# Output projection of an attention block: two fp32 products a tile in place of six products of high and low parts

## The chip, the cores and the metric

The kernel runs on one core of a Trainium2 chip. The metric is device time of one execution in microseconds. The profile shows one execution, its engines (PE is TensorE's matmul, PEld its load of weights, DVE VectorE, ACT ScalarE, POOL GpSimd, SP the queue that issues DMAs) and the granted clock of TensorE.

## What is computed

Three layers on 8 x 576 tokens of width 512: chunked attention in 8 heads, a mixture of four attention experts of head size 64, and a normed MLP. The change touches the second one; from its reference:

```python
for e in range(E):
    q = x @ wq[e]; k = x @ wk[e]; v = x @ wv[e]
    scores = scale * (q @ k.transpose(0, 2, 1))
    scores = np.where(causal, -1000000000.0, scores)
    scores = scores - scores.max(-1, keepdims=True)
    a = np.exp(scores)
    a /= a.sum(-1, keepdims=True) + 1e-09
    ye = a @ v @ wo[e]
    for kk in range(K):
        mask = topk[:, :, kk] == e
        out += mask[..., None] * w[:, :, kk:kk + 1] * ye
```

All values are fp32. wo is (4, 64, 512).

## The kernel before

Tokens are cut into 36 tiles of 128, nine to a pair of batch rows. A step of the main loop (tick) works on several tiles at once: chunked attention of tile s, projections of a group of three tiles, and expert attention of tile g = s - 7. Within a step a written plan (PLAN, a string of letters) sets the order of the work on PE, DVE, ACT and POOL; S are scores, O the values step, T the transposes of the probabilities, Y the output projection, P projections, C the chunk products. The last steps, from 402 us on, run beside the start of the MLP, and there a scheduler orders the engines. The first tiles (the prologue) have an order string of their own, PRO, also left to the scheduler.

Large products are made at reduced precision (type F32R) from split operands: a value is written as a high part, rounded by ACT, and a low part, the rest, by DVE (split, lines 117 to 123), and a product is the sum of low x high, high x low and high x high. Other products, scores of the chunk layer (line 151), its values (187), expert values (428), take plain fp32 operands.

The expert values step (attn_values, from line 415) writes o_ps[128, 2, 128]: the rows are the 64 values of two experts, the columns 128 tokens, for two pairs of experts. Each product of line 428 fills one half of the rows of o_ps (64 of the array's columns) from pT, the transposed probabilities of 128 tokens. At line 431 ACT writes the high part zh from o_ps and DVE the low part zl. attn_out (from line 433) then makes, two steps of the plan later, y_ps[128, 512] of six products of 512 columns (line 438): for each pair of experts (zl, woh), (zh, wol), (zh, woh). ACT copies y_ps to y (line 443), and SP stores it to xs in DRAM (line 444), which the MLP reads.

The weight wo is loaded in the prologue through a tile of two slots (wraw, line 135) that also carries wk, wq and wv, and split into woh and wol. Names in the rows: xTh and xTl are the split outputs of chunked attention (line 196), the operands of the projections pp (246) and pv (273); P are the probabilities, tp and pTa their transposes (409, 411, 413); sx_ps, s_ps and pT_ps belong to chunked attention; conversions of the MLP's weights (narrow, from line 453) run on DVE and POOL beside all this.

Of the kernel before, what the change touches and what calls it, by code (L numbers as in the profile page):

```python
# [7 lines left out]
F32 = mybir.dt.float32  # L8
F32R = mybir.dt.float32r
BF16 = mybir.dt.bfloat16  # L10
AF = mybir.ActivationFunctionType
OP = mybir.AluOpType
# [10 lines left out]
def tile_kernel(ctx, tc, dims, qkt, vt, wqt, wkt, wvt, wo, g_ln, w_ch1, w_ch2, out):  # L23
    nc = tc.nc
    B, H, S, D = dims
    E, HD, DM = wo.shape
# [8 lines left out]
    EP = E // 2  # L35
# [4 lines left out]
    VW = NV + E  # L40
# [14 lines left out]
    def f32(ap):  # L55
        return ap.bitcast(F32)
# [10 lines left out]
    se = early.enter_context(tc.tile_pool(name="se", bufs=1, side="right"))  # L67
    sa = late.enter_context(tc.tile_pool(name="sa", bufs=1))
# [42 lines left out]
    wkl = sp_.tile([128, KF, NV], F32R)  # L111
    wvh = sp_.tile([128, KF, VW], F32R)
    wvl = sp_.tile([128, KF, VW], F32R)
    woh = sa.tile([128, EP, DM], F32R)
    wol = sa.tile([128, EP, DM], F32R)

    def split(hi, lo, src, sc=None):
        if sc is None:
            nc.scalar.activation(hi, src, AF.Copy)
            nc.vector.tensor_tensor(lo, src, f32(hi), OP.subtract)  # L120
        else:
            nc.scalar.activation(hi, src, AF.Copy, scale=sc)
            nc.vector.scalar_tensor_tensor(lo, src, sc, f32(hi), OP.mult, OP.subtract)

    def load_w():
        for hi, lo, src, sc in ((wkh, wkl, wkt, None), (wqh, wql, wqt, qscale), (wvh, wvl, wvt, None)):
            w = src.shape[2]
            for half in range(2):
                fs = slice(half * 2, half * 2 + 2)
                raw = se.tile([128, 2, VW], F32, name="wraw", bufs=2)  # L130
                nc.sync.dma_start(raw[:, :, :w], src[:, fs, :])
                split(hi[:, fs, :], lo[:, fs, :], raw[:, :, :w], sc)
            yield
        for ep in range(EP):
            raw = se.tile([128, 2, VW], F32, name="wraw", bufs=2).rearrange("p a b -> p (a b)")[:, :DM]
            nc.sync.dma_start(raw, wo[2 * ep:2 * ep + 2].rearrange("e d n -> (e d) n"))
            split(woh[:, ep, :], wol[:, ep, :], raw)
        yield

    groups = {}  # L140
# [175 lines left out]
    Ps, pTs, zs, sums_ = {}, {}, {}, {}  # L316

    def split_of(g):
        p, t = divmod(g, PT)
        w = 0 if t <= 4 else 1  # L320
        n = t + 1 - 4 * w
        return p, t, w, n
# [92 lines left out]
    def attn_values(g):  # L415
        p, t, w, n = split_of(g)
        pT = pTs.pop(g)
        zh = sa.tile([128, EP, 128], F32R, name="zh", bufs=2)
        zl = sa.tile([128, EP, 128], F32R, name="zl", bufs=2)
        zs[g] = (zh, zl)  # L420
        o_ps = ps.tile([128, EP, 128], F32, name="oa_ps", tag="ps")
        for ep in range(EP):
            for kt in range(n):
                gk = p * PT + 4 * w + kt
                vg = vgs[gk // GT]
                for e2 in range(2):
                    e = 2 * ep + e2
                    nc.tensor.matmul(o_ps[e2 * HD:(e2 + 1) * HD, ep, :], vg[:, gk % GT, e * HD:(e + 1) * HD],  # L428
                                     pT[:, e * n + kt, :], start=(kt == 0), stop=(kt == n - 1),
                                     skip_group_check=True)  # L430
        return (lambda: nc.scalar.activation(zh, o_ps, AF.Copy)), (lambda: nc.vector.tensor_tensor(zl, o_ps, f32(zh), OP.subtract))

    def attn_out(g):
        zh, zl = zs.pop(g)
        y_ps = ps.tile([128, DM], F32, name="y_ps", tag="ps")
        for e2 in range(EP):
            for i, (a, b_) in enumerate(((zl, woh), (zh, wol), (zh, woh))):
                nc.tensor.matmul(y_ps, a[:, e2, :], b_[:, e2, :], start=(e2 == 0 and i == 0),  # L438
                                 stop=(e2 == EP - 1 and i == 2))
        y = sa.tile([128, DM], F32, name="y", bufs=1)  # L440

        def send():
            nc.scalar.activation(y, y_ps, AF.Copy)
            nc.sync.dma_start(xs[g // 2][:, g % 2, :], y)

        return send
# [105 lines left out]
    def tick(s, fill=None):  # L552
# [39 lines left out]
        def values():  # L592
            do["Z"], do["z"] = attn_values(g - 2)

        def out_():
            do["y"] = attn_out(g - 2)
# [33 lines left out]
    TAIL = NT + 4  # L630
    projs = []
    weights = load_w()


# [4 lines left out]
    for op in PRO.split():  # L639
        c, n = op[0], int(op[1:] or 0)  # L640
# [303 lines left out]
    n = len(seq) - 1  # L944
# [181 lines left out]
```

## Time and profile before

| what | value |
|---|---|
| median of 3 runs | 1214.92 us (1214.33 to 1216.7) |
| profiled execution | 1214.83 us, its span 1213.1 us |
| mean granted clock of TensorE | 0.993 |
| PE busy | 1182.9 us, 98% of the span |
| DVE, ACT, POOL busy | 903.9, 581.7, 267.8 us |
| chain that ended last | 86% PE, 7% DVE, 3% DMA |

Busy time of an engine is the union of its instructions' spans. Ends of matmuls are modelled, so the pace of a row of products is read from their starts: a row of the timeline gives start, duration, engine, line, operation, tiles and shapes, and in brackets the idle time before it and who ended it. Merged rows carry a count (x4). The chain is followed back from the last instruction, and its pieces are given in order of time.

### The profile page before, as it was taken

What the parts mean: (1) busy time and instruction counts of PE and PEld (TensorE: products, weight loads), DVE (VectorE), ACT (ScalarE), POOL (GpSimd) and SP (SyncE); (2) the same over time, 40 slices, a digit from 0 to 9 for tenths busy, and PEclk for the clock granted to TensorE, in tenths of its full rate; (3) what the DMA queues carried; (4) which work ended last, traced back from release to release, by engine and by line L of the source; (5) the groups of instructions that cost most, each with busy time, mean ns of one, the idle gap of its engine ahead of it and who ended that gap; (6) DMA issues with size and microseconds to landing.
All of it is one profiled execution on the core that took longest, in us unless ns stands there. A gap on an engine that the chain in (4) does not pass through costs nothing.

```text
span 1213.1 us, 29176 instructions
## 1 busy us (share of the span) xinstructions
PE 1182.9 (98%) x11874; PEld 1130.0 (93%) x11874; DVE 903.9 (75%) x1837; ACT 581.7 (48%) x1117; POOL 267.8 (22%) x480
## 2 busy tenths in 40 slices
PE   7989999999999999999999999998999999999998
PEld 5879998999999888999999999998999999999998
DVE  5688888888887769865775676456997777876882
ACT  3466566666666776433433343345543343333440
POOL 2245445544545333111111211110000000000000
PEclk8989999999999999999999999999999999999999
DMA  8334343434332246655455545558855545455431
GB/s 284 103 108 141 134 152 115 145 129 146 130 102 75 77 146 228 199 177 178 159 181 183 178 161 175 171 172 284 296 177 165 165 147 167 157 157 168 146 105 35
DMA packets 95845, 191.69 MB, mean 158 GB/s; under 512 B 8544, under 2 KB 42336, under 8 KB 94816
## 3 DMA queue, kind: packets, MB, share of 16 engines
q1 hardware_dynamic: 95712, 189.83, 47.2%
q8 instruction: 93, 1.52, 0.5%
q14 instruction: 40, 0.33, 0.1%
HBM read 118.50 MB, written 71.30 MB: 156 GB/s over the span
## 4 chain that ended last, share of the span: by engine, by line
PE 86%; DVE 7%; DMA 3%; ACT 1%; issue 1%; POOL 1%; SPq 0%; ACTq 0%; DVEq 0%; POOLq 0%
PE bb L1023 16%; PE bb L833 16%; PE ad L1023 12%; PE ad L833 12%; PE pp L246 7%; PE pv L273 4%; PE y_ps L438 4%; PE oa_ps L428 4%; PE tp L409 3%; PE sp L358 3%; PE tp L724 2%; PE sx_ps L151 1%; DMA w2u<-w2d 1%; PE pT_ps L177 1%; DVE P L376 1%; PE sx_ps L187 1%
## 5 line engine op out<-in xcount | busy, mean ns | idle before, releaser
L833 PE MATMUL bb<-x,w1u 128*128 128x256 f32 x1728 | 217.2, 281 | 2.4 <-ACT p L854 1.5
L833 PEld LDWEIGHTS bb<-x,w1u 128*128 128x128 f32 x1728 | 209.7, 188 | 3.6 <-ACT p L854 2.1
L833 PE MATMUL ad<-x,w1u 128*128 128x256 f32 x1296 | 173.4, 283 | 0.7 <-DVE v L857 0.7
L833 PEld LDWEIGHTS ad<-x,w1u 128*128 128x128 f32 x1296 | 160.5, 188 | 1.0 <-DVE v L857 0.8
L1023 PE MATMUL bb<-w2u,hn 128*128 128x256 f32 x928 | 159.9, 280 | 0.8 <-DVE xr L1033 0.8
L1023 PEld LDWEIGHTS bb<-w2u,hn 128*128 128x128 f32 x928 | 134.0, 189 | 1.0 <-DVE xr L1033 1.0
L1023 PE MATMUL bb<-w2u,hx 128*128 128x256 f32 x640 | 125.9, 283 | 0.4 <-DVE hx L988 0.4
L381 ACT ACTIVATE P<-P,nm 128x128 f32<-128x128 f32 (+8 forms) x144 | 87.2, 608 | 44.3 <-DVE nm L376 37.0
L1023 PE MATMUL ad<-w2u,hn 128*128 128x256 f32 x632 | 104.4, 281 | 0.0
L398 POOL TENSOR_SCALAR P<-P,l 128x128 f32<-128x128 f32 (+8 forms) x144 | 94.8, 676 | 39.7 <-DVE l L391 24.9
L1023 PEld LDWEIGHTS bb<-w2u,hx 128*128 128x128 f32 x640 | 101.2, 191 | 0.6 <-DVE hx L988 0.6
L479 POOL TENSOR_TENSOR cvt<-cva,cvt 128x512 f32<-128x512 f32 x32 | 44.3, 1385 | 239.8 <-DVE cvt L475 203.2
L1023 PEld LDWEIGHTS ad<-w2u,hn 128*128 128x128 f32 x632 | 89.3, 189 | 0.0
L1023 PE MATMUL ad<-w2u,hx 128*128 128x256 f32 x504 | 88.9, 280 | 0.0
L509 POOL TENSOR_TENSOR cw<-cw 128x128 f32<-128x128 f32 x128 | 64.8, 526 | 57.7 <-issue 48.4
L1023 PEld LDWEIGHTS ad<-w2u,hx 128*128 128x128 f32 x504 | 74.1, 189 | 0.0
L171 POOL TENSOR_TENSOR pc<-pc,lc 128x512 f32<-128x512 f32 x36 | 37.8, 1052 | 140.0 <-DVE lc L167 83.1
L376 DVE CUSTOM_DVE_ANT_0 P<-sp,mcaus 128x128 f32<-128x128 f32 (+7 forms) x128 | 59.8, 516 | 3.7 <-PE sp L358 3.6
L742 DVE TENSOR_TENSOR x<-xt,x 128x512 fp32r<-128x512 f32 x63 | 46.2, 742 | 19.5 <-ACT x L741 19.3
L428 PE MATMUL oa_ps<-pTa,vg 128*64 128x128 f32 x928 | 59.6, 277 | 0.3 <-DVE pTa L413 0.3
L409 PE MATMUL tp<-ident,P 128*128 128x128 f32 x464 | 57.9, 274 | 1.4 <-POOL P L398 1.3
L409 PEld LDWEIGHTS tp<-ident,P 128*128 128x128 f32 x464 | 52.0, 141 | 4.8 <-POOL P L398 1.8
(244 smaller groups left out, 2588.9 us busy)
## 6 DMA issues: line engine op xcount, KB each, us to landing
qk<-in_qk SPq DMA_DIRECT2D x36, 512.0 KB, 4.5
hn<-hd SPq DMA_DIRECT2D x34, 512.0 KB, 4.4
raw<-in_w_ch SPq DMA_DIRECT2D x32, 512.0 KB, 3.7
hx<-hd SPq DMA_DIRECT2D x29, 512.0 KB, 4.6
vb<-in_v SPq DMA_DIRECT2D x36, 256.0 KB, 4.4
xs<-y SPq DMA_DIRECT2D x36, 256.0 KB, 2.1
xc<-xs SPq DMA_DIRECT2D x18, 512.0 KB, 4.5
hd<-p SPq DMA_DIRECT2D x36, 256.0 KB, 3.8
```

Source lines behind the costliest of these rows:

```text
L246: nc.tensor.matmul(pp, a[:, f, ws], b_[:, f, :], start=(f == 0 and n == 0), stop=(f == KF - 1 and n == 2))
L273: nc.tensor.matmul(pv, a[:, f, cs], b_[:, f, :], start=(f == 0 and n == 0), stop=(f == KF - 1 and n == 2))
L376: nc.vector.tensor_tensor_reduce(dst, src, mk, -1.0, -3.0 * NEG, OP.add, OP.min, nm[:, e2:e2 + 1])
L381: nc.scalar.activation(pe, pe, AF.Exp, bias=nm[:, e2:e2 + 1], scale=-1.0, accum_out=l[:, e2:e2 + 1])
L398: nc.gpsimd.tensor_scalar(pe, pe, sums_[g][:, ep, e2:e2 + 1], 1.0, OP.mult, OP.mult)
L409: nc.tensor.transpose(tp[:, i, :], P[ep][e2][:, kt * 128:(kt + 1) * 128], ident)
L428: nc.tensor.matmul(o_ps[e2 * HD:(e2 + 1) * HD, ep, :], vg[:, gk % GT, e * HD:(e + 1) * HD], pT[:, e * n + kt, :], start=(kt == 0), stop=(k ...
L438: nc.tensor.matmul(y_ps, a[:, e2, :], b_[:, e2, :], start=(e2 == 0 and i == 0), stop=(e2 == EP - 1 and i == 2))
L509: nc.gpsimd.tensor_tensor(w[:, o, :], w[:, x, :], w[:, y, :], op)
L742: nc.vector.tensor_tensor(t[:, 1], tsum[i], f32(t[:, 0]), OP.subtract)
L833: nc.tensor.matmul(out[:, p], w[:, kt, a, WI[i], :], x[:, b_, kt, :], start=(start and p == 0 and kt == 0 and q == 0), stop=False, skip_gr ...
L1023: ins = nc.tensor.matmul(to[:, t], x[:, c, ts], w2u[i][:, w, half * 4 + c, :], start=start, stop=False, skip_group_check=True)
```

## The change

The high and low copies of wo and of the expert values go. wo is loaded straight into one fp32 tile (wof) that keeps its place, ACT copies o_ps into one fp32 tile z, DVE's subtraction is dropped, and y_ps is the sum of two fp32 products of 512 columns.

```diff
-    woh = sa.tile([128, EP, DM], F32R)
-    wol = sa.tile([128, EP, DM], F32R)
+    wof = sa.tile([128, EP, DM], F32)
...
         for ep in range(EP):
-            raw = se.tile([128, 2, VW], F32, name="wraw", bufs=2).rearrange("p a b -> p (a b)")[:, :DM]
-            nc.sync.dma_start(raw, wo[2 * ep:2 * ep + 2].rearrange("e d n -> (e d) n"))
-            split(woh[:, ep, :], wol[:, ep, :], raw)
+            nc.sync.dma_start(wof[:, ep, :], wo[2 * ep:2 * ep + 2].rearrange("e d n -> (e d) n"))
...
-        zh = sa.tile([128, EP, 128], F32R, name="zh", bufs=2)
-        zl = sa.tile([128, EP, 128], F32R, name="zl", bufs=2)
-        zs[g] = (zh, zl)
+        z = zs[g] = sa.tile([128, EP, 128], F32, name="z", bufs=2)
...
-        return (lambda: nc.scalar.activation(zh, o_ps, AF.Copy)), (lambda: nc.vector.tensor_tensor(zl, o_ps, f32(zh), OP.subtract))
+        return (lambda: nc.scalar.activation(z, o_ps, AF.Copy)), (lambda: None)
...
-        zh, zl = zs.pop(g)
+        z = zs.pop(g)
         y_ps = ps.tile([128, DM], F32, name="y_ps", tag="ps")
         for e2 in range(EP):
-            for i, (a, b_) in enumerate(((zl, woh), (zh, wol), (zh, woh))):
-                nc.tensor.matmul(y_ps, a[:, e2, :], b_[:, e2, :], start=(e2 == 0 and i == 0),
-                                 stop=(e2 == EP - 1 and i == 2))
+            nc.tensor.matmul(y_ps, z[:, e2, :], wof[:, e2, :], start=(e2 == 0), stop=(e2 == EP - 1))
```

In the steps of the plan nothing else moves. TensorE's order around an output projection of the main loop, before (tp are the transposes of the next tile's probabilities, pp a projection):

```order
L246 MATMUL pp<-xTh,wkh 128x384
L409 MATMUL tp<-ident,P 128x128 x12
L438 MATMUL y_ps<-woh,zl 128x512
L438 MATMUL y_ps<-wol,zh 128x512
L438 MATMUL y_ps<-woh,zh 128x512
L438 MATMUL y_ps<-woh,zl 128x512
L438 MATMUL y_ps<-wol,zh 128x512
L438 MATMUL y_ps<-woh,zh 128x512
L246 MATMUL pp<-xTl,wqh 128x384
```

and the same place now:

```order
L243 MATMUL pp<-xTh,wkh 128x384
L406 MATMUL tp<-ident,P 128x128 x12
L432 MATMUL y_ps<-wof,z 128x512 x2
L243 MATMUL pp<-xTl,wqh 128x384
L243 MATMUL pp<-xTh,wql 128x384
```

Six products became two in the same place, between the same neighbours. In the prologue the scheduler's order changes. VectorE's order ahead of the first projection, before (pc is the shifted scores of a chunk, xTl the last operand that the first projection needs):

```order
L155 TENSOR_REDUCE nmc<-s_ps 128x8
L157 TENSOR_TENSOR pc<-s_ps,nmc 128x2x4x64
L120 TENSOR_TENSOR wol<-wraw,woh 128x512
L196 TENSOR_TENSOR xTl<-x_ps,xTh 128x4x128
L165 TENSOR_REDUCE lc<-pc 128x8
L120 TENSOR_TENSOR wol<-wraw,woh 128x512
```

and now:

```order
L152 TENSOR_REDUCE nmc<-s_ps 128x8
L154 TENSOR_TENSOR pc<-s_ps,nmc 128x2x4x64
L193 TENSOR_TENSOR xTl<-x_ps,xTh 128x4x128
L162 TENSOR_REDUCE lc<-pc 128x8
L163 TENSOR_SCALAR lc<-lc 128x8
```

xTl follows the shift directly. SP's queue in the prologue, before (raw is the first load of the MLP's weights, in 64-bit form):

```order
L104 DMA qk<-in_qk 128x1024
L459 DMA raw_816<-in_w_ch 128x1024
L105 DMA vb<-in_v 128x512
L131 DMA wraw<-in_wv 128x520 x2
L104 DMA qk<-in_qk 128x1024
L105 DMA vb<-in_v 128x512
L136 DMA wraw<-in_wo 128x512 x2
L104 DMA qk<-in_qk 128x1024
```

and now:

```order
L104 DMA qk<-in_qk 128x1024
L134 DMA wof<-in_wo 128x512
L105 DMA vb<-in_v 128x512
L130 DMA wraw<-in_wv 128x520 x2
L134 DMA wof<-in_wo 128x512
L104 DMA qk<-in_qk 128x1024
L105 DMA vb<-in_v 128x512
L452 DMA raw_809<-in_w_ch 128x1024
```

The two loads of wo no longer wait for a slot and stand on both sides of those of wv; the load of raw moved behind them.

## Rows read from the trace of the kernel before

**Rows 1.** Busy time by stage (us), and TensorE's clock in 40 slices.
```profile
70.00:400.00 330.00, 329.04 (x4304) 298.78 (x4300) 276.42 (x790) 209.04 (x527) 166.62 (x309) 1.00 0.36 125
400.00:470.00 70.00, 65.42 (x581) 55.88 (x577) 55.28 (x161) 52.12 (x114) 23.61 (x53) 1.00 0.36 124
...
PEclk8989999999999999999999999999999999999999
```
**Rows 2.** Waits of PE from 70 to 475 us: total, times, longest.
```profile
PE y_ps L438 <- DVE zl L431: 2.2, 3, 1.2
PE tp L409 <- POOL P L398: 1.3, 2, 0.9
PE sp L358 <- DVE pTa L413: 1.1, 1, 1.1
PE tp L724 <- DVE zl L431: 0.4, 1, 0.4
```
**Rows 3.** Instructions of tile y_ps in both stages: PE, PEld, ACT busy.
```profile
70.00:400.00 330.00, 45.87 (x168) 29.45 (x168) 16.72 (x28) 1.00 0.36 125
400.00:470.00 70.00, 13.33 (x48) 8.33 (x48) 4.81 (x8) 1.00 0.36 124
```
**Rows 4.** Timeline of PE in one tile: second product, and what follows the sixth.
```profile
268.10 0.39 PE L438 MATMUL y_ps<-wol,zh 128*128 128x512 f32 x1
...
269.26 0.33 PE L246 MATMUL pp<-xTl,wqh 128*128 128x384 f32 x1
```
**Rows 5.** Timeline of PE, values step, windows ending at 261.64, 261.75, 261.97.
```profile
261.57 0.33 PE L428 MATMUL oa_ps<-pTa,vg 128*64 128x128 f32 x2
261.57 0.44 PE L428 MATMUL oa_ps<-pTa,vg 128*64 128x128 f32 x4
261.57 0.66 PE L428 MATMUL oa_ps<-pTa,vg 128*64 128x128 f32 x8
```
**Rows 6.** Timeline of PE: chunk products on quarters of the array.
```profile
260.48 0.69 PE L151 MATMUL sx_ps<-qk 64*64 64x64 f32 x32
261.00 0.65 PE L187 MATMUL sx_ps<-pTc,vb 64*64 64x64 f32 x32
```
**Rows 7.** Timeline of PE: first projections behind a values step.
```profile
276.35 0.44 PE L246 MATMUL pp<-xTl,wkh 128*128 128x384 f32 x1
276.63 0.34 PE L246 MATMUL pp<-xTh,wkl 128*128 128x384 f32 x1
276.81 0.34 PE L246 MATMUL pp<-xTh,wkh 128*128 128x384 f32 x1
```
**Rows 8.** A timeline row of PE, and tile zl: ns min/median/max, first and last start.
```profile
194.40 0.50 PE L438 MATMUL y_ps<-woh,zl 128*128 128x512 f32 x1 [0.77 <-DVE zl L431]
...
L431 DVE TENSOR_TENSOR zl<-oa_ps,zh x36: 371/413/426, 74.2 to 466.2; 128x256 fp32r<-128x256 f32 x36
```
**Rows 9.** The chain that ended last, in the prologue: start, us.
```profile
24.75 2.97 DMA wraw<-in_wo
...
29.75 2.38 PE pp L246 x12
```
**Rows 10.** Timeline of the prologue: VectorE's shift and TensorE's transposes.
```profile
27.55 0.69 DVE L157 TENSOR_TENSOR pc<-s_ps,nmc 128x512 f32<-128x512 f32 x1
...
28.15 0.66 PE L177 MATMUL pT_ps<-ident,pc 128*128 128x128 f32 x4 [1.13 <-POOL pc L171]
```
**Rows 11.** The chain from 400 to 470 us: zl in it.
```profile
414.37 0.32 DVE zl L431
...
445.70 0.33 DVE zl L431
...
452.00 0.40 DVE zl L431
```
**Rows 12.** Timeline of the loads of weights (PEld) in the first tile.
```profile
76.96 0.19 PEld L438 LDWEIGHTS y_ps<-wol,zh 128*128 128x128 f32 x1
77.19 0.19 PEld L438 LDWEIGHTS y_ps<-woh,zh 128*128 128x128 f32 x1
```

## The prediction

> **What bounds the kernel now.** I read the table by stage first, with the clock of the forty slices beside it. Between 70 and 400 us TensorE is busy for 329.04 of 330 us at a full granted clock [rows 1], so every nanosecond that the change adds there on TensorE comes out at the end, and VectorE (276 us busy) has room. From 400 to 470 us TensorE is busy for 65.42 of 70 us; there other engines own a part of the path. The waits say whose: TensorE waited 2.2 us in three waits of y_ps for zl, 1.3 us for GpSimd's probabilities, 1.1 us for pTa, 0.4 us behind zl once more [rows 2]. The output projection runs 28 times in the first stretch (168 products) and 8 times in the second (48) [rows 3]. After 470 us nothing of it runs, and what follows moves as a block. The profiled execution took 1214.83 us (span 1213.1), the median of three runs is 1214.92; the sum is made on 1214.83.
>
> **What one tile costs today.** Products of y_ps start at 268.10 (the second of six) and the next step's first product at 269.26 [rows 4]: five products in 1.16 us, 0.232 us each, 1.39 us for six. Loads of weights lie under them.
>
> **What one tile will cost.** The new products are plain fp32 on the whole array, 512 columns, two a tile. No such row is in the trace, so I bound them. The nearest is oa_ps, the values step: plain fp32, 128 columns, into one half of the array's columns. Line 428 issues 464 of them and the trace has 928 records, so one fp32 product is two records. Counted from 261.57 in windows that end later and later, two records have started by 261.64, four by 261.75, eight by 261.97, and the form's time goes from 0.33 over 0.44 to 0.66 us [rows 5]: records start in pairs, 0.11 us apart. A pair is the two halves of the array's columns, and whether the halves run side by side decides everything. If they do, each needs 0.11 us for 128 columns, two cycles a column at 2.4 GHz; if they only start together and share the time, one cycle. The scores of line 151 speak for side by side: 32 records of 64 columns on quarters of the array start at 260.48 and the next form at 261.00 [rows 6], 16 ns a record, where 64 columns one after the other would take 27 ns at 2.4 GHz. I take two cycles a column: a record of 512 columns is four times 0.109 less a little fixed time, 0.43 us, four of them 1.72 us. That is **0.33 us more a tile**.
> The bounds: below, the halves sharing the time, 0.055 us per 128 columns and record, 4 x 0.23 = 0.92 us, 0.47 us less a tile; that is a case of its own, the first rival. Above, the pace of the reduced-precision rows, 0.232 us for one pass of 512 columns, for both passes: 4 x 0.464 = 1.86 us, 0.47 us more; and a load of weights that is not hidden where the form changes. After oa_ps the first product takes 276.63 - 276.35 = 0.28 us and the next 0.18 [rows 7], so 0.10 us of load shows; before y_ps, behind whole-array transposes, none does. I take none after y_ps, since there too the array is used whole, and keep 0.57 us a tile as the upper end.
> On the reading of the pair a page decides the same way: the Trainium skill, FP8 and Floating Point Precision, section TensorE Precision Notes, has true fp32 as four passes through the array. By it two records carry two passes each and the sum stays; by the pair step of the row, read as halves that share the time, the tile would be shorter by 0.47 us.
>
> **70 to 400 us.** 28 tiles x 0.33 = +9.2 us, all on the path. Of the waits for zl one lies here, 0.77 us before the tile at 194.40 [rows 8]: z is drained by ScalarE alone now, the subtraction on VectorE (36 x 0.41 us [rows 8]) is gone, and TensorE no longer waits for its turn in VectorE's queue. -0.8. The drain itself is the same ScalarE step in the same place, and what stands behind the waiting product on TensorE is the next transposes or projections, which now wait only for ScalarE. Next late is TensorE itself.
>
> **The prologue.** Before, the split of wo sits on the path: its raw tile waits for a slot, the load lands at 27.7, then come ScalarE's high part, VectorE's wol, xTl, and the first projection at 29.75 [rows 9]. Without it VectorE goes from the shift that ends at 28.24 straight to xTl (0.6 us), and TensorE is free at 28.75, when the transposes from 28.15 end [rows 10]; ScalarE's xTh, which stood behind woh, comes earlier as well. The projection can start at 28.85: -0.9 us. On SP's queue the first load of wo moves ahead of vb and wv, and the 512 KB load of raw channel weights moves behind both; less stands ahead of wv and the chain in rows 9 isn't held by raw, so I cost the moves at nothing. Their bounds are 0.7 us either way, a quarter of the 2.97 us that one load of this size takes from issue to landing.
>
> **400 to 470 us.** Eight tiles. I follow the chain.
> - The first two tiles lie beside 1.2 + 1.1 us of TensorE's idle time, waiting for zl and for pTa [rows 2]; the path there is VectorE's, shorter by the 0.32 us of zl at 414.37 [rows 11].
> - The third tile costs +0.33.
> - The wait of 0.4 us behind zl [rows 2] goes, the fourth tile adds 0.33.
> - The fifth and sixth tile lie beside the 1.3 us that TensorE waits for GpSimd [rows 2]; the path is again VectorE's and loses 0.33 and 0.40 us [rows 11].
> - The last two tiles add 0.66.
>
> Together -0.32 + 0.33 - 0.4 + 0.33 - 0.73 + 0.66 = -0.1 us. If nothing is given back it is +2.6, if every shortening counts and the last tiles hide too, -1.5. The scheduler also writes the layer norm's small steps earlier in VectorE's order here and drops two table loads on ScalarE; I cost it at nothing inside these bounds.
>
> **Stores.** At four places the store of y changes places with a store or load of other data on SP. y has one buffer, but tiles are 330 / 28 = 11.8 us apart [rows 3] and a load of the same 256 KB takes 2.97 us [rows 9], so nothing waits; if that cover went, a tile would be late by one such store.
>
> **Sum.** +9.2 - 0.8 - 0.9 - 0.1 = +7.4 us: 1214.83 + 7.4 = **1222.2 us**, 0.6% slower. A difference under 0.2% (2.4 us) can't be told from none with this kernel.
>
> **Rivals.**
> - *One pass a record: faster.* If the halves of oa_ps share the time and the quarters' rows mean only that the two row halves overlap, an fp32 product costs half of what I took: 36 x -0.47 = -16.9 us on TensorE, of which VectorE's path keeps back some 2 between 400 and 470. It decides at 0.35 us a record (four records equal to today's 1.39). For it: row halves alone would allow 13 ns a record in rows 6, and 16 was seen. Against it: the two records of a pair start together in rows 5, and the records of whole-array forms never do. It gives about 1198. Chance 0.05.
> - *Loads bound the step: faster.* If TensorE's pace were set by loading weights, 144 loads instead of 216, at the 0.10 us that one shows where it is not hidden [rows 7], would save 72 x 0.10 = 7.2 us, and with the other gains the time would be near 1206. Against it: in y_ps the loads stand 0.23 us apart [rows 12], at the pace of the products and not at their own. Chance 0.02. The Trainium skill, Perfetto Trace Analysis, section Identifying the Most-Contended Engine, has the busy share of LDWEIGHTS and not that of the matmuls as the measure of TensorE's headroom, which by its 93% here would speak for the change; the rows just named speak against using it for this step.
> - *The cover is larger than I think: no change.* If the loss between 70 and 400 us stays at 9.2 but the prologue gives 1.6, the waits 1.2 and the last stretch 4, the rest is 2.4 us, the edge of what can be told: 1217. For it: VectorE loses 14.8 us of work. Against it: VectorE isn't waited for in that stretch but once. Chance 0.04.
> - *Dearer records.* The reduced-precision pace for both passes, or an unhidden load after each tile: 0.43 to 0.57 us a tile, 28 x 0.1 to 0.24 = 2.8 to 6.7 us on top, and up to 2 more in the last stretch: 1225 to 1231. Chance 0.14.
>
> My forecast has 0.75. The clock adds a spread of its own: in two of the page's forty slices, 0 to 30 and 61 to 91 us, the granted clock is under 0.9 [rows 1], so a part of each ran at the lower level, 1.2 GHz, behind idle stretches of the prologue. Where such a part ends once the prologue is shorter may move the time by 1 to 2 us either way.
>
> **Range and chances.** 1217.5 to 1230: the low end is the forecast with the gains of the prologue and the last stretch at their bounds and the clock's 2 us, the high end takes in most of the dearer records; about 0.2 is left out. Faster 0.07, same 0.04, slower 0.89.
>
> **What would show it.** In the profile after: y_ps with 144 records (four a tile) about 0.43 us apart, a tile at 1.72 us; TensorE still busy for all of the stretch after 70 us, which is longer by 28 x 0.33; no idle time before y_ps; the first projection near 28.9 us. The drain of the last tile, whose subtraction now starts at 466.2 [rows 8], should come about 7 us later, and the rest after it be as long as before. If records are 0.23 us apart the first rival holds; if the first product behind y_ps shows 0.10 us more, the dearer case.

## The result, and the profile after

The changed kernel is slower, as forecast. Four runs of it have a median of 1225.91 us (1223.03 to 1226.61) against 1215.61 us for the kernel before: a ratio of 1.0081 (95% interval 1.0061 to 1.0100). In a second measurement six runs gave 1223.55 us against 1215.81, a ratio of 1.0062 (1.0048 to 1.0077). So the change costs 7.5 to 10 us by these ratios; forecast were 7.4, and a time of 1222.2 us in a range of 1217.5 to 1230. The profiled execution took 1225.92 us, its span is 1224.2.

The page, engines and TensorE's clock in 40 slices:

```profile
PE 1193.1 (97%) x11802; PEld 1115.6 (91%) x11802; DVE 890.3 (73%) x1799; ACT 578.8 (47%) x1113; POOL 271.3 (22%) x480
...
PEclk9999999999999999999999999999999999999999
```

TensorE is busy for 10.2 us more than before (1182.9) with 72 records fewer; VectorE for 13.6 us less. The work that VectorE lost was hidden, the work that TensorE got was not.

Busy time of the two stages, which answer to [rows 1] (columns: PE, PEld, DVE, ACT, POOL busy, granted clock, DMA share, GB/s):

```profile
70.00:410.00 340.00, 339.40 (x4268) 289.80 (x4266) 271.86 (x771) 211.81 (x531) 167.88 (x315) 1.00 0.36 122
410.00:480.00 70.00, 67.04 (x555) 52.13 (x555) 52.42 (x159) 50.20 (x112) 23.68 (x48) 1.00 0.38 130
```

The first stretch is again all TensorE, at a full clock; in the second TensorE idles for 3.0 us, where it was 4.6.

One tile of the new output projection, in windows of the timeline of PE that end at 272.3, 272.7, 273.1 and 273.55, and the projection behind it; then the group of all of them on the page (count, busy us, mean ns, idle before):

```profile
272.18 0.59 PE L432 MATMUL y_ps<-wof,z 128*128 128x512 f32 x1
272.18 1.02 PE L432 MATMUL y_ps<-wof,z 128*128 128x512 f32 x2
272.18 1.45 PE L432 MATMUL y_ps<-wof,z 128*128 128x512 f32 x3
272.18 1.88 PE L432 MATMUL y_ps<-wof,z 128*128 128x512 f32 x4
...
274.07 0.33 PE L243 MATMUL pp<-xTh,wql 128*128 128x384 f32 x1
...
L432 PE MATMUL y_ps<-wof,z 128*128 128x512 f32 x144 | 68.8, 598 | 0.1
```

Four records a tile, each adding 0.43 us. The form's time grows from 0.59 to 1.88 us in three steps; a tile is 4 x 0.43 = 1.72 us, where six products took 1.39 [rows 4]. The second projection behind it starts 1.89 us after the first record, which is the tile and one projection step of 0.175 us: no load of weights shows.

PE's waits from 70 to 485 us, in place of [rows 2]:

```profile
PE tp L406 <- POOL P L395: 1.8, 2, 0.9
PE pp L243 <- DVE ql L261: 1.0, 1, 1.0
PE pp L243 <- DVE kWl L261: 0.5, 1, 0.5
```

The waits of y_ps are gone. Two others stand in their place.

Where the time came from, by stretches between starts of products in the trace. The kernel before was profiled three times and the changed one three times; all six are shown, since one execution alone misleads in two of the rows. "28th tile" is the output projection's, "MLP start" the 33rd record on w1u, the MLP's first weights, "boundary" the stretch from the 2905th of them to the 121st record on w2u, the second ones:

| stretch, us | before | after | mean difference |
|---|---|---|---|
| start to the first y_ps | 76.87, 77.68, 76.96 | 76.74, 75.09, 77.54 | -0.7 |
| first y_ps to the 28th tile | 318.00, 317.74, 318.05 | 326.05, 326.05, 326.31 | +8.2 |
| 28th tile to MLP start | 76.27, 76.53, 76.52 | 77.09, 77.03, 77.16 | +0.7 |
| MLP start to the 2905th record | 359.3, 358.0, 358.5 | 359.1, 358.6, 358.1 | 0.0 |
| boundary | 35.4, 35.8, 35.5 | 37.7, 37.9, 36.2 | +1.7 |
| the rest | 347.25, 347.26, 347.26 | 347.46, 347.16, 347.26 | 0.0 |

The sum is +9.9 us, as the six profiled times differ on average (1224.6 against 1214.7).

### The profile page after: what moved, and what is told of

Same layout as the page of the kernel before. It is cut to its first block, busy times and chain, and to the rows that moved or that the text cites. A ratio compares the mean times of both kernels' runs of the same rounds, so it can differ in the third digit from the quotient of the medians.

```text
span 1224.2 us, 28990 instructions
## 1 busy us (share of the span) xinstructions
PE 1193.1 (97%) x11802; PEld 1115.6 (91%) x11802; DVE 890.3 (73%) x1799; ACT 578.8 (47%) x1113; POOL 271.3 (22%) x480
## 4 chain that ended last, share of the span: by engine, by line
PE 88%; DMA 4%; DVE 4%; ACT 2%; POOL 1%; issue 1%; SPq 0%; ACTq 0%; DVEq 0%; POOLq 0%
PE bb L1016 16%; PE bb L826 15%; PE ad L1016 12%; PE ad L826 11%; PE pp L243 8%; PE y_ps L432 5%; PE oa_ps L423 4%; PE pv L270 4%; PE tp L406 4%; PE sp L355 4%; DMA w2u<-w2d 2%; PE tp L717 2%; PE sx_ps L148 1%; PE pT_ps L174 1%; PE sx_ps L184 1%
## 5 line engine op out<-in xcount | busy, mean ns | idle before, releaser
L472 POOL TENSOR_TENSOR cvt<-cva,cvt 128x512 f32<-128x512 f32 x32 | 46.8, 1464 | 238.6 <-DVE cvt L468 217.6
L432 PE MATMUL y_ps<-wof,z 128*128 128x512 f32 x144 | 68.8, 598 | 0.1
L735 DVE TENSOR_TENSOR x<-xt,x 128x512 fp32r<-128x512 f32 x63 | 45.4, 731 | 19.0 <-ACT x L734 19.0
```

The lines of the kernel that those rows point to most:

```text
L432: nc.tensor.matmul(y_ps, z[:, e2, :], wof[:, e2, :], start=(e2 == 0), stop=(e2 == EP - 1))
```

## The experiments

Ratios are to the kernel before on the same chip. The changed kernel's second measurement, the doubled products, the subtraction and the weight's preparation ran on one chip, the three that start from fewer or reordered products on another.

**The changed kernel again.** No edit; a second measurement and a second profile.

> The changed kernel once more. In its first profile the attention stage ended 7.9 us later than before (first product of the MLP behind the last output projection at 476.45 instead of 468.57), and the whole run 11.1 us later: some 3 us came after, around 836 to 865 us, between the two halves of the MLP, where TensorE waits for ScalarE behind a load of w2u. Theory: those 3 us depend on how loads fall in that execution and are not tied to the change; then this profile again has 7.5 to 8.5 us at the end of the attention stage, but another length between the halves, and the time is 8 to 11 us over before. Rival: the longer stretch between the halves belongs to the changed order of loads and comes again in full, with the time 10 to 11 us over.

Measured: 1223.55 us, ratio 1.0062 (1.0048 to 1.0077). The main stretch, from the first output projection to the 28th, is 326.05 us as in the first profile. The difference of the medians is +7.7 us, below the bounds of both theories, and the boundary came again at full length (37.9 us), against the theory and as the rival had it. The first output projection lies 1.65 us earlier than in the first profile.

**Twice the products.** Each product of the output projection is issued twice and the copy halves the sum, so a tile has eight records:

```diff
-            nc.tensor.matmul(y_ps, z[:, e2, :], wof[:, e2, :], start=(e2 == 0), stop=(e2 == EP - 1))
+            for i in range(2):
+                nc.tensor.matmul(y_ps, z[:, e2, :], wof[:, e2, :], start=(e2 + i == 0), stop=(e2 + i == EP))
...
-            nc.scalar.activation(y, y_ps, AF.Copy)
+            nc.scalar.activation(y, y_ps, AF.Copy, scale=0.5)
```

> Every product of the changed output projection is issued twice, and y is scaled by a half: eight records a tile instead of four, nothing else. Theory (a whole-array fp32 record of 512 columns takes 0.43 us, all of it on the path): 1.72 us more a tile, 28 x 1.72 = 48 us from 70 to 400 us and most of 8 x 1.72 = 14 us after, so 56 to 62 us over the changed kernel, near 1285. Rival (a part of each tile is fixed cost at the change of form, or lies in waits): 45 us or less over the changed kernel.

Measured: 1281.81 us, 58.3 more than the changed kernel on that chip; ratio 1.0542 (1.0521 to 1.0563). Its group on the page and the stage (columns as above):

```profile
L433 PE MATMUL y_ps<-wof,z 128*128 128x512 f32 x288 | 130.5, 595 | 0.0
...
70.00:445.00 375.00, 374.92 (x4244) 302.54 (x4243) 264.66 (x744) 207.19 (x517) 161.53 (x303) 1.00 0.31 109
```

The main stretch is 371.45 us, 45.4 more than 326.05 for 27 tiles: 1.68 us for four records, 0.42 each. So a record costs on the path about what the rows' steps say (the changed kernel's one wait of 0.5 us in this stretch is gone here; with it the four records cost 1.70), and what is added to TensorE shows in full in this stage's time. Busy time in that group is 130.5 us for 288 records, 0.45 each, while the mean duration of one is 595 ns: the mean of a pipelined record is not its price.

**VectorE's subtraction put back.** It writes a tile zl that nothing reads:

```diff
+        zl = sa.tile([128, EP, 128], F32R, name="zl", bufs=2)
...
-        return (lambda: nc.scalar.activation(z, o_ps, AF.Copy)), (lambda: None)
+        return (lambda: nc.scalar.activation(z, o_ps, AF.Copy)), (lambda: nc.vector.tensor_tensor(zl, o_ps, z, OP.subtract))
```

> The changed kernel with VectorE's subtraction put back (36 of about 0.41 us) into a tile that nobody reads; TensorE still waits for ScalarE's z alone. Theory (TensorE bounds 70 to 400 us, VectorE matters only in the last stretch of the attention): 0.3 to 1.5 us over the changed kernel, all of it between 400 and 480 us. Rival (VectorE's relief gave back several us of the dearer products): 3 us or more over the changed kernel.

Measured: 1224.66 us, ratio 1.0066 (1.0049 to 1.0083), against 1223.55 without it: the intervals overlap. Main stretch 326.44 us (326.05 to 326.31 without), last stretch 76.52 (77.03 to 77.16 without). So 14.9 us of VectorE's work are worth 0.1 to 0.4 us in the main stretch and nothing in the last, where the expectation had put all of its 0.3 to 1.5 us. It showed something else. One row of PE's timeline, the subtraction on VectorE's, and the copy to z on ScalarE's:

```profile
198.12 1.12 PE L433 MATMUL y_ps<-wof,z 128*128 128x512 f32 x2 [0.63 <-DVE zl L427]
...
197.65 0.41 DVE L427 TENSOR_TENSOR zl<-oa_ps,z 128x256 fp32r<-128x256 f32 x1
...
195.69 0.36 ACT L427 ACTIVATE z<-oa_ps 128x256 f32<-128x256 f32 x1
```

The product waits for zl though it reads only z and wof, and z was done at 196.05. What zl still holds is oa_ps: y_ps, oa_ps and other tiles share two buffers (tag "ps"), and oa_ps comes free when its last reader is done.

**zl last.** The kernel before, with the four products that need only zh first:

```diff
-            for i, (a, b_) in enumerate(((zl, woh), (zh, wol), (zh, woh))):
-                nc.tensor.matmul(y_ps, a[:, e2, :], b_[:, e2, :], start=(e2 == 0 and i == 0),
-                                 stop=(e2 == EP - 1 and i == 2))
+            for i, b_ in enumerate((wol, woh)):
+                nc.tensor.matmul(y_ps, zh[:, e2, :], b_[:, e2, :], start=(e2 == 0 and i == 0), stop=False)
+        for e2 in range(EP):
+            nc.tensor.matmul(y_ps, zl[:, e2, :], woh[:, e2, :], start=False, stop=(e2 == EP - 1))
```

> The kernel before with its six products in another order: the four with zh first, the two with zl last, so that TensorE begins a tile without waiting for VectorE's zl; nothing else. Theory (of the wait for zl, 2.2 us of TensorE's idle time is given back where TensorE bounds, as in the changed kernel): attention stage 0.8 to 2 us shorter than 391.5, time 1 to 2 us under before. Rival (the wait is absorbed by the next one): within 0.3 us.

Measured in 11 runs: 1213.55 us, ratio 0.9979 (0.9970 to 0.9988), the only version of the same computation that beats both kernels. But the wait that it was meant to cover is still there. A row of PE's timeline, and PE's waits from 70 to 475 us:

```profile
195.88 0.50 PE L438 MATMUL y_ps<-wol,zh 128*128 128x512 f32 x1 [0.79 <-DVE zl L431]
...
PE y_ps L438 <- DVE zl L431: 2.0, 2, 1.2
PE sp L358 <- DVE pTa L413: 1.1, 1, 1.1
PE tp L725 <- DVE zl L431: 0.4, 1, 0.4
```

The first product reads zh, and it waits for zl for 0.79 us, where 0.77 stood in [rows 8]. Together with the run before this says that the buffer alone is enough to hold TensorE there, whether or not the first product reads zl. The main stretch is unchanged (317.74 us, against 317.74 to 318.05). The gain lies in the last stretch, 74.26 us against 76.27 to 76.53, where the waits for GpSimd's P (1.3 us) and for pTa before oa_ps are gone; there the scheduler chose another order. The time is 3.2 us under before on that chip (1216.71), more than the 1 to 2 us of the theory, and not from the place that it named. That the later use of zl is worth anything by itself isn't shown.

**Two reduced-precision products.** z and wo are rounded to F32R and the low parts left out of the result; two products of 512 columns a tile, one record each:

```diff
-    wof = sa.tile([128, EP, DM], F32)
+    wof = sa.tile([128, EP, DM], F32R)
...
-        z = zs[g] = sa.tile([128, EP, 128], F32, name="z", bufs=2)
+        z = zs[g] = sa.tile([128, EP, 128], F32R, name="z", bufs=2)
```

> Two reduced-precision products a tile, from z and wo both rounded and without their low parts: the low parts' products are left out. The work beside it is as in the changed kernel (no subtraction on VectorE), wo goes through the two-slot tile again. Theory (TensorE's time for the tile is what counts, one cycle a column for this form): 0.46 us a tile, 0.93 less than before and 1.26 less than the changed kernel; attention stage 25 us shorter from 70 to 400 us, as long as no other engine takes over, up to 30 in all, time near 1188. Rival (VectorE, busy for 276 of 330 us, or another engine becomes the bound): 15 us or less.

Measured: 1201.26 us, ratio 0.9877 (0.9858 to 0.9896). The main stretch is 306.15 us, 11.8 less than before; four products fewer in each of 27 tiles, at 0.232 us, would be 25 less. The time is 15.4 us under before (1216.71), about at the rival's bound and far from the theory's 1188. PE's waits from 70 to 470 us say what came in between:

```profile
PE pp L245 <- DVE kWl L263: 4.9, 4, 1.9
PE pv L272 <- DVE kWl L263: 2.9, 3, 1.2
PE pv L272 <- ACT y L438: 2.3, 3, 0.8
PE tp L408 <- POOL P L397: 1.7, 3, 1.0
PE tp L408 <- DVE nm L375: 1.7, 1, 1.7
PE sp L357 <- DVE pTa L412: 1.3, 1, 1.3
```

A stage whose TensorE is busy for 329 of 330 us has other engines close behind it. Less work on TensorE gave back half of its price here, more work cost all of it.

**Four products.** The kernel before without the products on wol (the low part of the weight is left out of the result):

```diff
-            for i, (a, b_) in enumerate(((zl, woh), (zh, wol), (zh, woh))):
-                nc.tensor.matmul(y_ps, a[:, e2, :], b_[:, e2, :], start=(e2 == 0 and i == 0),
-                                 stop=(e2 == EP - 1 and i == 2))
+            for i, a in enumerate((zl, zh)):
+                nc.tensor.matmul(y_ps, a[:, e2, :], woh[:, e2, :], start=(e2 == 0 and i == 0),
+                                 stop=(e2 == EP - 1 and i == 1))
```

> The kernel before without the products with wol: four reduced-precision products a tile of zl and zh with the rounded wo; the weight's low part is left out of the product. Theory: 0.93 us a tile, 0.46 less than before, 28 x 0.46 = 13 us from 70 to 400 us and up to 3 after, time 1199 to 1203. Rival (another engine bounds): 8 us or less.

Measured: 1204.11 us, ratio 0.9901 (0.9885 to 0.9918). Main stretch 311.54 us, 6.4 less than before, where two products in each of 27 tiles would be 12.5; last stretch 5.2 less. The time is 12.6 us under before on that chip, a little over the range expected. The waits of y_ps for zl grew from 2.2 us [rows 2]:

```profile
PE y_ps L438 <- DVE zl L431: 3.1, 4, 1.6
```

It is the same half again.

**The weight's preparation put back into the prologue.** Beside the direct loads, wo is loaded through wraw and split again, into tiles that nothing reads:

```diff
+    woh = sa.tile([128, EP, DM], F32R)
+    wol = sa.tile([128, EP, DM], F32R)
...
+            raw = se.tile([128, 2, VW], F32, name="wraw", bufs=2).rearrange("p a b -> p (a b)")[:, :DM]
+            nc.sync.dma_start(raw, wo[2 * ep:2 * ep + 2].rearrange("e d n -> (e d) n"))
+            split(woh[:, ep, :], wol[:, ep, :], raw)
             nc.sync.dma_start(wof[:, ep, :], wo[2 * ep:2 * ep + 2].rearrange("e d n -> (e d) n"))
```

> The changed kernel with the loads of wo through the two-slot tile and their split by ScalarE and VectorE put back into the prologue, into tiles that nobody reads, beside the new direct loads: only the prologue's gain is undone. Theory: the first projection starts 0.6 to 0.9 us later and so does the first output projection, 0.3 to 1 us over the changed kernel; where the clock falls in the prologue may hide it. Rival (the prologue gained nothing): same time within 0.3 us, first projection at the same time.

Measured: 1227.94 us, ratio 1.0097 (1.0082 to 1.0112), 4.4 us more than the changed kernel on that chip. Timelines of its prologue, VectorE and PE:

```profile
30.54 0.69 DVE L121 TENSOR_TENSOR wol<-wraw,woh 128x512 fp32r<-128x512 f32 x1 [1.48 <-ACT woh L120]
31.15 0.69 DVE L198 TENSOR_TENSOR xTl<-x_ps,xTh 128x512 fp32r<-128x512 f32 x1
...
31.89 0.69 PE L248 MATMUL pp<-xTl,wkh 128*128 128x384 f32 x1 [2.25 <-DVE xTl L198]
```

The split stands ahead of xTl on VectorE again, and the first projection starts at 31.89 us instead of 28.95 to 29.30. Expected were 0.6 to 0.9 us; it is 2.6 to 2.9, and the first output projection, at 80.64 us, comes over 3 us later than in any profile of the changed kernel. With two loads of wo more than either kernel this is dearer than the kernel before (29.75 to 30.11), so it shows the place and the sign of the prologue's gain, not its size.

**The kernel before again, and a third profile of each.** No edits.

> The kernel before once more, for a second profile. In its first one the MLP's first half (from the end of the last output projection to its 2880th product) took 358.9 us and the stretch from there to the 120th product of the second half 38.6 us; two profiles of the changed kernel have 359.8 to 360.3 and 40.6 to 40.8, some 3 us more in all, four profiles of its relatives 358.9 to 360.5 and 38.9 to 39.6. Theory (these stretches differ by execution, through loads and the clock): the second profile of before has another value in them, between 358.5 and 361 and between 38 and 41. Rival (the changed order of loads makes them longer): the same 358.9 and 38.6 within 0.3 us. The attention stage, from the first output projection to the end of the last, should be the same in either case, 391.5 us within 0.3.

> The changed kernel once more, one profile, for the stretch between the two halves of the MLP (from the start of the 2904th product of the first half's matmuls to the 120th of the second half's): 37.8 and 38.0 us in the two profiles of the changed kernel, 35.4 and 35.8 in two of the kernel before, though behind the last output projection the order of all engines is the same in both. If the changed kernel makes the stretch longer (its loads fall at another point of the transfers before them), the stretch is again 37.5 to 38.2 us. If transfers merely land earlier or later from execution to execution, it may come out anywhere from 35.4 to 38. The main stretch (first to 28th output projection) is 326.05 us again by both.

> The kernel before once more, one profile. By the first theory (the change lengthens the stretch between the MLP's halves) the stretch is 35.3 to 36 us again; by the second (spread between executions) it may come out up to 38. The main stretch is 317.7 to 318.0 us by both.

Measured: 1214.67, 1224.27 and 1214.51 us; the stretches are those of the table. The second profile of the kernel before differs from its first by -1.3 us in the MLP's first half and by +0.3 at the boundary, so these stretches do differ between executions, though the first half fell below the bounds expected. The boundary was the question of the third profiles: 36.2 us in the third profile of the changed kernel, below the bounds expected of the theory that the change lengthens it, and 35.5 in that of the kernel before, no wider than it had been. The instructions of all five engines stand in the same order in both kernels from some 45 us behind the last output projection on (VectorE's fall into step last, at 513 us of before), over 300 us ahead of this boundary, so no step of the change is there. TensorE's waits near the end of the MLP's first half, of before (828 to 850 us) and of after (837 to 860, first and third profile):

```profile
PE bb L833 <- ACT v L854: 0.8, 1, 0.8
```

```profile
PE bb L826 <- ACT p L847: 1.4, 1, 1.4
PE bb L826 <- ACT v L847: 1.4, 1, 1.4
```

```profile
PE bb L826 <- ACT v L847: 1.8, 1, 1.8
```

In ScalarE's queue conversions of w2u stand ahead of p and v, and they wait for the load. One of them in the timeline of ACT, of before and of after:

```profile
833.91 0.63 ACT L885 ACTIVATE w2u<-w2u 128x512 fp32r<-128x512 f32 x1 [1.16 <-DMA w2u<-w2d]
```

```profile
845.01 0.63 ACT L878 ACTIVATE w2u<-w2u 128x512 fp32r<-128x512 f32 x1 [3.79 <-DMA w2u<-w2d]
```

From issue to landing (the last number, median us) these loads took, in the same windows of before and after:

```profile
w2u<-w2d SPq DMA_DIRECT2D x2, 1024.0 KB, 5.9
```

```profile
w2u<-w2d SPq DMA_DIRECT2D x2, 1024.0 KB, 8.6
```

The other profiles have 5.8 and 5.7 us for before, and 7.7 and 7.1 for after. The granted clock plays a part too. Busy time over the boundary (columns as above), in the first profile of before and the first and second of after:

```profile
830.40:865.90 35.50, 30.52 (x241) 29.75 (x241) 27.06 (x34) 18.58 (x27) 0.00 (x0) 0.95 0.91 311
```

```profile
839.00:876.80 37.80, 29.75 (x243) 28.48 (x241) 26.55 (x33) 17.48 (x26) 0.00 (x0) 1.00 0.88 305
```

```profile
836.80:874.80 38.00, 32.15 (x243) 31.27 (x242) 26.42 (x33) 17.57 (x25) 0.00 (x0) 0.87 0.85 283
```

In the first profile of the changed kernel TensorE idles for 3 us more than before, at a full clock. In the second it idles for 0.9 more and is busy for 1.6 more, at a granted clock of 0.87 instead of 0.95. So two boundaries of nearly the same length have different causes. Kernels with the same order there spread between these: 36.1 us with the subtraction put back, 36.8 with the weight split again, 36.7 with the products doubled, 36.4 with zl last, 37.3 with four products, 35.8 with two. Spread between executions is part of it; whether the changed kernel's loads also meet other transfers at this point stays open.

## Why the prediction was right

**A record of 0.43 us.** Measured 0.429 from the rows and 0.42 on the path. The reading that decided it, that the two records of a pair in [rows 5] run side by side on halves of the array and each needs two cycles a column, holds for the whole array: 512 columns at two cycles and 2.4 GHz are 0.427 us. Two records of it make a product of four cycles a column. The Trainium skill, FP8 and Floating Point Precision, section TensorE Precision Notes, has true fp32 as four passes through the array; the measured 0.86 us, four cycles a column, agrees with it if a pass takes one cycle a column. One pass a record, the first rival, falls; so do the dearer records: 0.43 and not 0.46, and no load behind the tile.

**The main stretch.** Forecast for the 27 tiles between the first and the 28th: 27 x 0.33 - 0.77 = +8.1 us. Measured +8.2. That the two agree to 0.1 us is in part luck. The wait of 0.77 us ahead of one tile went, but its reason was put too simply (the subtraction held oa_ps's buffer, which keeps TensorE waiting even where the product doesn't read zl), and next late was not TensorE itself. In the changed kernel the same place reads, PE first and then VectorE:

```profile
196.21 1.88 PE L432 MATMUL y_ps<-wof,z 128*128 128x512 f32 x4
198.61 0.44 PE L243 MATMUL pp<-xTl,wqh 128*128 128x384 f32 x1 [0.52 <-DVE kWl L261]
...
198.05 0.51 DVE L261 TENSOR_TENSOR kWl<-pp,kWh 128x384 fp32r<-128x384 f32 x1
```

TensorE starts the tile without waiting and then stands 0.52 us for VectorE's kWl, two steps further in the same queue. Of 0.77 us gained 0.25 are left. The tile's price was also a little high: 4 x 0.429 - 1.392 = 0.324. With both put right the sum is 27 x 0.324 - 0.25 = +8.5; where the other 0.3 us went was not followed.

**The last stretch.** Forecast -0.1 us for eight tiles, or +0.2 with the 28th tile that the table counts here; measured +0.7. The step that failed is the idle time that the change was to give back: nine tiles add 2.9 us, and the shortened chains of VectorE were to give 2.7 back. But TensorE's waits in this stretch fell only from 4.5 us to 2.8: those for zl and pTa went, GpSimd's P grew from 1.3 to 1.8, and 1.0 for ql appeared. That accounts for 1.2 us of loss; the 0.5 us of it that don't show were not followed. Pieces of the chain that ended last, start and us:

```profile
419.23 0.48 DVE ql L261
...
437.00 1.72 PE y_ps L432 x4
...
458.87 5.14 DMA w1u<-w1d
464.03 1.80 ACT w1u L678 x2
465.92 4.06 POOL P L395 x2
```

and GpSimd's piece in the chain of before:

```profile
458.86 2.29 POOL P L398 x2
```

Ahead of the last two tiles the path runs over a load, ScalarE and 4.06 us of GpSimd, 2.29 before, in which VectorE's subtraction has no part. The run with it put back agrees: nothing is lost here.

**The prologue.** Forecast -0.9 us at the first projection. Measured 29.13, 28.95 and 29.30 against 29.75, 30.11 and 29.86: -0.8. The chain that ended last no longer holds the load of wo:

```profile
24.92 0.70 DVE wvl L119
...
28.48 0.61 DVE xTl L193
...
29.13 3.91 PE pp L243 x12
```

The twelve projections take 3.91 us here and 2.38 in [rows 9]. That is the clock:

```profile
29.50:32.80 3.30, 3.30 (x12) 3.06 (x10) 0.74 (x3) 0.25 (x1) 1.04 (x1) 0.50 0.13 46
```

The granted clock was 0.50, the level of 1.2 GHz. In the second profile of the same kernel the same stretch ran at 1.00:

```profile
29.50:32.80 3.30, 3.30 (x48) 2.99 (x47) 1.28 (x5) 1.16 (x3) 1.04 (x1) 1.00 0.09 32
```

There the first output projection came at 75.09 us instead of 76.74. What TensorE did ahead of the projections was nearly the same in both profiles, first and second:

```profile
20.00:29.10 9.10, 5.98 (x158) 4.82 (x156) 6.10 (x12) 3.94 (x7) 1.73 (x2) 1.00 0.93 307
```

```profile
20.00:28.95 8.95, 6.06 (x159) 4.88 (x157) 6.15 (x12) 3.98 (x7) 1.78 (x2) 1.00 0.93 315
```

So why the clock fell in the one and not in the other isn't shown. The spread of 1 to 2 us that the forecast allowed is there, and the -0.7 us at the first output projection are not clear of it; the -0.8 at the first projection are.

**After 470 us.** "What follows moves as a block" held for the MLP's halves (0.0 us both) and not for the boundary between them, 1.7 us longer on average. This part of the difference was put at nothing in the forecast and isn't fully explained. With 0.5 from the last stretch and 0.2 from the prologue it makes nearly all of the 2.5 us by which the six profiles differ by more (9.9) than the forecast (7.4).

**The other rivals.** Loads bound the step: the busy share of LDWEIGHTS fell from 93% to 91% with the 72 loads, and the time rose; from 70 to 410 us it is 85% (289.8 of 340 us), while TensorE has no idle time to speak of. The Trainium skill, Perfetto Trace Analysis, section Identifying the Most-Contended Engine, takes the busy share of LDWEIGHTS, beside the share of peak FLOPs, as the measure of TensorE's headroom; by that share alone one would have gone the wrong way here. The steps between starts of records pointed the right way. No change: VectorE's cover was worth some tenths.

## What to carry to other kernels

Price a product by the steps between starts of records, not by their mean duration or by the count of instructions: on this chip two plain fp32 products (1.72 us a tile) cost more than six of split operands (1.39). Where one engine is busy all of a stage, what is added to it costs its full price; what is taken away may give less, here about half, before the next engine is late. A wait that names a tile can be for the buffer which that tile's writer reads; moving the use of the tile then gains nothing at that place.

## What was not expected of the hardware

- An fp32 product of 128 by 512 on the whole array is two records of 0.429 us; one at reduced precision is one record of 0.232 us. Split into three it costs 0.70 us, whole 0.86. The prediction had worked out 0.43 from smaller records; no row of before showed it.
- The prologue's stretches at the lower clock lie elsewhere in each execution of one kernel: the first projections took 0.32 us apart in one profile of the changed kernel and 0.175 in another, which moved the first output projection by 1.7 us.
- Loads of 1 MB took from 5.7 to 8.6 us from issue to landing, as median of two in each profile, at a place where the instructions of all engines stand in the same order.
